# Retention attention and a Fourier-mixing block: a second fold of the channel axis, with step two of the channel transform in four half-contraction products

## The chip, the cores and the metric

The kernel runs on one core of a Trainium2 chip. The core has five engines, each with its own in-order queue of instructions: TensorE (PE in the profile, with its weight loads shown apart as PEld), VectorE (DVE), ScalarE (ACT), GpSimd (POOL) and SyncE (SP, which here only issues DMAs). The metric is the time on the device of one execution in microseconds (us). SBUF is the memory [...]; PSUM is where PE puts its products, and DVE and ACT fetch them from there.

## The reference

For each of 4 batches and 8 heads, with a sequence S of 768 and a head size D of 64:

```python
gamma = 1.0 - 2.0 ** (-5.0 - np.arange(H))
for t in range(S):                               # attention with a decaying state
    state = gamma * state + k[t] v[t]^T          # D x D for each head
    y[t] = scale * q[t] state
x = y.transpose(0, 2, 1, 3).reshape(B, S, H * D) # (4, 768, 512)
mixed = real(fft(fft(x, axis=1), axis=2))        # over the sequence and the channels
u = x + mixed
un = (u - mean(u)) / sqrt(var(u) + 1e-6)         # over the 512 channels
out = u + relu(un @ w_ch1) @ w_ch2               # 512 -> 2048 -> 512
```

(The attention is abbreviated: the head and batch indices are left out.)

## The kernel before

The work is done batch by batch, and everything of PE runs in fp16 with fp32 sums. Per batch there are four head pairs of attention and then the mixing block.

**Attention.** For each head pair, `cast_unit` (L233) turns q, k and v into fp16 on POOL (k also scaled, L253), `t_unit` transposes q and k (L278), `a0_unit` and `a_unit` (L299, L317) form masked products of q and k, `kv_unit` (L335, L345) updates the state, `y_unit` (L366, L370) forms the output in PSUM, and ACT scales it into the fp16 tile `x` (L378).

**The transform.** The sequence is folded first: `fold_s` (L395, DVE) adds and subtracts rows s and s + 384 into the tile `ab`. Then `fold_d` (L405, DVE) folds the channels, d with 512 - d, into `eo`: even sums (e = 0) for the cosine part and odd differences (e = 1) for the sine part, 256 channels in two halves `cb` of 128. `g0_unit` (L443 to L462) treats the channel that has no partner. Step one, `s1_unit` (L425), transforms the sequence: per half and part six matmuls of 193 columns against the tables `csp` or `ssp`, into the PSUM tile `ps1`; ACT (L437) or DVE (L439) copies it as fp16 into `g`, and a DVE copy reversed along the row makes `gr` (L440), which serves the mirrored upper three row blocks. Step two, `s2_unit` (L467), transforms the channels: for each of six row blocks `kb` of 128 rows, two matmuls of 257 columns against the cosine table `cd16` are summed in the first 257 columns of a PSUM tile `pq` (called `psP`), and two of 255 columns against the sine table `sd16` in the other 255 (`psQ`). ACT copies `psQ` to SBUF (`qn`, L488), and DVE writes the sum and the reversed difference of both as the row block of `u` (L491, L493). Then x is added to both halves: the lower one at L497 (DVE in batch 0, POOL later), the upper one at L500 (POOL, but DVE in batch 0 from block 3 on).

**Normalisation and the two dense layers.** DVE takes the mean and variance of u (L510, L511), ACT subtracts the mean into `un` (L506 for the first three blocks of batch 0, with a mean from elsewhere, L512 otherwise), PE transposes it and ACT or DVE copies that as `unT` (`unT_unit`, L533). `h_unit` (L556) makes the hidden layer in 16 groups of four matmuls of 384 columns, `ht` being written alternately by ACT (L560) and DVE (L562); for the lower half of batch 0 `h0_unit` (L573) does so for each row block with matmuls of 128 columns. `ch_unit` (L593) makes the output layer, 192 matmuls of 512 columns a batch in groups of four, and DVE (L597) adds u; then the block is stored.

**What sets the order.** Functions ending in `_unit` return small pieces of work. For each batch the kernel makes streams: the dense layers (`majors`), step two and normalisation of the upper three row blocks (`mix_units`), and, for the next batch, loads, attention (`attn_steps`, L621) and step two of its first three blocks. A stream has a start and an end time in units of a batch, `emit` spaces its pieces evenly between these, sorts all by due time and calls them in that order. The framework's scheduler then orders each engine's queue from that, so an added piece can move others. `attn_steps` has six steps, and the loop runs pair i through them: `y_unit(b, i)` in step i + 2. The first fold, g0 and the two step-one units of half 0 stand at i = 2, that is behind the third head pair; those of half 1 in step 5, behind the fourth.

**Loads and constants.** Loads of q, k, v are issued by SP in turn (`load_unit`, L96). Those of batch 1 wait until the last of eight weight chunks has landed (the argument `after` = 7); the weight chunks are issued from POOL's queue behind the last casts of batch 0 (L607, L615). In `late_consts` (L153) ACT scales a mask eight times, behind the `un` of row block 2 of batch 0. The tables csp, ssp, cd16 and sd16 are computed at the start by DVE and ACT.

**Buffers.** Of PSUM, five buffers (`ps_g`) serve steps one and two and the attention, three (`ps_pm`) the dense layers. `ab` and `eo` have one buffer each.

Of the kernel before, what the change touches and what calls it, by code (L numbers as in the profile page):

```python
# [12 lines left out]
ALU = mybir.AluOpType  # L13
# [21 lines left out]
def kernel(  # L35
# [45 lines left out]
    gk128 = const.tile([P, NHP], f32, tag="gk128")  # L81
    pmask = const.tile([P, 4], f32, tag="pmask")
    sgn = const.tile([P, 1], f32, tag="sgn")

    in_of = {}
    w_dma = []
# [63 lines left out]
    def late_consts():  # L150
        with tc.issue_after(lb[0]["una"].ins):
            for h in range(H):
                nc.scalar.activation(maskp[:, h // 2, h % 2], maskf, AF.Copy, bias=0.0,  # L153
                                     scale=float(gam[h] ** (-P)))
        for j in range(2):
            nc.vector.memset(qzs[j][:, :, 0, D:P], 0.0)
            nc.vector.memset(qzs[j][:, :, 1, 0:D], 0.0)

    m2 = const.tile([P, 1], f32, tag="m2c")
    odd = const.tile([P, 1], f32, tag="oddc")  # L160
# [239 lines left out]
    def fold_d(b, cb):  # L400
# [6 lines left out]
                                        in1=ab[:, :, :, 1, i0:i0 + 128], op=op)  # L407
        return run

    def xmean_unit(kb):  # L410
        def run():
            if kb == 0:
                fd[0]["xm"] = stt.tile([P, 4], f32, tag="xm", name="xm")
            junk = up.tile([P, 2, 257], f16, tag="un16", name="junk")
            nc.scalar.activation(junk, xts[0][:, kb, :, 1:258], AF.Copy, bias=0.0, scale=1.0,
                                 accum_out=fd[0]["xm"][:, kb:kb + 1])
        return run
# [7 lines left out]
    def s1_unit(b, e, cb):  # L425
        def run():
            eo, g, gr = fd[b]["eo"], fd[b]["g"], fd[b]["gr"]
            tab = csp if e == 0 else ssp
            ps = ps_g.tile([P, 2, NK], f32, tag="g", name="ps1", padded_shape=[P, 2, 256])
            for par in range(2):  # L430
                for sb in range(3):
                    nc.tensor.matmul(ps[:, par, :], eo[:, e, par, sb, 128 * cb:128 * cb + 128],  # L432
                                     tab[:, par, sb, :], start=(sb == 0), stop=(sb == 2))
            gi = 2 * e + cb
            dst = g[:, gi].rearrange("p (i t) -> p t i", t=2)
            if e == 0 or b == 0:
                nc.scalar.copy(dst, ps)  # L437
            else:
                nc.vector.tensor_copy(dst, ps)  # L439
            nc.vector.tensor_copy(gr[:, gi], g[:, gi, 384:0:-1])  # L440
        return run

    def g0_unit(b):  # L443
        def run():
            ab = fd[b]["ab"]
            xg = stt.tile([P, 3, 4], f16, tag="xg", name="xg")
            src = ab[:, :, :, 0, 1].rearrange("p a c -> p c a")
            nc.vector.tensor_copy(xg[:, :, 0:2], src)
            nc.vector.tensor_scalar(out=xg[:, :, 2:4], in0=src, scalar1=sgn, scalar2=None,
                                    op0=ALU.mult)  # L450
            ps = ps_g.tile([P, 3, 4], f32, tag="g", name="ps0", padded_shape=[P, 3, 160])
            for kb in range(3):
                for sb in range(3):
                    nc.tensor.matmul(ps[:, kb, :], csn[:, sb, P * kb:P * kb + P], xg[:, sb, :],
                                     start=(sb == 0), stop=(sb == 2))
            gm = stt.tile([P, 3, 4], f32, tag="gm", name="gm")
            nc.vector.tensor_tensor(out=gm, in0=ps,
                                    in1=pmask.unsqueeze(1).to_broadcast([P, 3, 4]), op=ALU.mult)
            g0 = stt.tile([P, 2, 3], f32, tag="g0", name="g0")
            nc.vector.tensor_tensor(out=g0.rearrange("p a k -> p k a"), in0=gm[:, :, 0:4:2],  # L460
                                    in1=gm[:, :, 1:4:2], op=ALU.add)
            fd[b]["g0"] = g0.rearrange("p a k -> p (a k)")  # L462
        return run
# [3 lines left out]
    def s2_unit(b, kb):  # L467
        def run():
# [9 lines left out]
            g0 = f["g0"][:, kb:kb + 1]  # L478
            pq = ps_g.tile([P, DM], f32, tag="g", name="pq")
            psP, psQ = pq[:, 0:257], pq[:, 257:512]  # L480
            for cb in range(2):
                nc.tensor.matmul(psP, gt[:, cb, j0:j0 + P], cd16[:, cb, :],
                                 start=(cb == 0), stop=(cb == 1))
            for cb in range(2):
                nc.tensor.matmul(psQ, gt[:, 2 + cb, j0:j0 + P], sd16[:, cb, 1:256],
                                 start=(cb == 0), stop=(cb == 1))
            qn = qns[kb % 2]
            nc.scalar.copy(qn[:, 1:256], psQ)  # L488
            op_lo = ALU.subtract if mirror else ALU.add
# [131 lines left out]
    def attn_steps(b):  # L621
        steps = []
        for step in range(6):
            un = []
            i = step - 2
            if 0 <= i < 4:
                un.append(y_unit(b, i))
                if i == 2:
                    un += [fold_s(b, 0, 130, 0, 2), fold_d(b, 0), g0_unit(b), s1_unit(b, 0, 0),
                           s1_unit(b, 1, 0)]  # L630
            if step < 4:
                un += [cast_unit(b, step), t_unit(b, step)]
            i = step - 1
# [3 lines left out]
                else:  # L637
                    un += [a_unit(b, i, 0), kv_unit(b, i), a_unit(b, i, 1), a_unit(b, i, 2)]
            if step == 5:
                un += [fold_s(b, 130, 258, 0, 2), fold_d(b, 1), s1_unit(b, 0, 1),  # L640
                       s1_unit(b, 1, 1)]
            steps.append(un)
        return steps
# [44 lines left out]
    for b in range(B):  # L688
# [15 lines left out]
        if b + 1 < B:  # L704
            steps = attn_steps(b + 1)
            if b == 0:
                streams.append(([load_unit(1, i, 7) for i in range(4)], -0.1, 0.0))
                ts = (0.12, 0.22, 0.24, 0.33, 0.42, 0.52, 0.59, 0.67)
            else:
                streams.append(([load_unit(b + 1, i) for i in range(4)], b - 0.3, b + 0.15))  # L710
# [37 lines left out]
```

## Time and profile before

| | us |
|---|---|
| three runs | 275.24, 274.93, 273.69 (median 274.93) |
| the profiled execution | 274.87 |
| its span, from its first instruction to its last | 273.1 |
| PE busy | 243.8 (89%) |
| DVE busy | 179.8 (66%) |
| ACT busy | 116.6 (43%) |
| POOL busy | 71.9 (26%) |

Every duration below is from one profiled execution, whose own time of 274.87 us is 1.77 us longer than its span; the mean granted clock of PE was 0.994 of full. Busy time of PE is the sum of modelled lengths of overlapping matmuls, so 89% doesn't mean that 11% are the whole that could be gained. A line of a timeline gives the start in us, the length in us, engine, line of the code, operation, what is written from what with sizes, and how many instructions are run together in it; in square brackets stand the idle time before it and what ended that. In a group's line, the busy time of all and the mean length of one in ns stand after the first bar, the engine's idle time just before them after the second.

The largest groups by engine are the output layer (L593, 90.4 us on PE), the hidden layer (84.0), DVE's `ht` (30.6) and ACT's (27.3). Of the rest, these are used below:

| group | count | mean of one, ns |
|---|---|---|
| ACT L378, x from PSUM | 32 | 585 |
| POOL L497, add of x | 18 | 637 |
| POOL L500, add of x | 21 | 650 |
| POOL L253, cast and scaling of k | 32 | 623 |
| POOL L258, cast of v | 16 | 834 |
| DVE L491, u from PSUM | 24 | 479 |
| DVE L510, statistics | 21 | 694 |

### The profile page before, as it was taken

To read this page: it belongs to the slowest core of one execution; us is meant where nothing else is said; L and a number is where in the kernel's file an instruction comes from. 1 tells how busy PE (TensorE), PEld (TensorE's weight loads), DVE (VectorE), ACT (ScalarE), POOL (GpSimd) and SP (SyncE) were. 2 spreads that over 40 slices of the span, in tenths; PEclk is the share of its full clock that TensorE was granted. 3 is DMA by queue.
4 is the path that set the end of the run, shared out by engine and by line. 5 is a ranking of instruction groups with operands and counts; after the bars stand their busy time and mean duration, and the time that the engine had idled before them with its cause. 6 is when DMAs were issued, how large, how long until landed. Compare 5 with 4: busy or idle time off the path is not lost.

```text
span 273.1 us, 5125 instructions
## 1 busy us (share of the span) xinstructions
PE 243.8 (89%) x1972; PEld 147.7 (54%) x1972; DVE 179.8 (66%) x458; ACT 116.6 (43%) x238; POOL 71.9 (26%) x122
## 2 busy tenths in 40 slices
PE   1498569998999998889999899989999999999994
PEld 0375458964456453556556544665566445545541
DVE  8964954986677676789778662699687736623411
ACT  3887456665554333546424540452234405402300
POOL 5769002565211214134402220510001303100000
PEclk9999997999999999999999999999999999999999
DMA  8999996999999597958996022144310131112012
GB/s 184 263 245 152 204 204 143 250 245 231 195 202 178 127 211 170 226 111 164 219 212 138 2 49 97 48 106 70 114 41 0 38 97 41 38 58 79 0 38 77
DMA packets 97432, 35.97 MB, mean 132 GB/s; under 512 B 88193, under 2 KB 94337, under 8 KB 97409
## 3 DMA queue, kind: packets, MB, share of 16 engines
q1 hardware_dynamic: 93184, 31.47, 54.2%
q0 software_dynamic: 4224, 4.19, 9.5%
q8 instruction: 15, 0.25, 0.4%
q14 instruction: 9, 0.07, 0.1%
HBM read 27.26 MB, written 6.29 MB: 123 GB/s over the span
## 4 chain that ended last, share of the span: by engine, by line
PE 56%; DVE 23%; ACT 7%; POOL 5%; issue 5%; DMA 1%; POOLq 0%; ACTq 0%; DVEq 0%
PE psc L593 25%; PE psh L556 14%; DVE bst L510 4%; PE ps L432 3%; POOL u L500 3%; PE wkY L366 2%; DVE u L491 2%; POOL u L497 2%; DVE xab L395 2%; PE tq L278 2%; PE psh L573 2%; PE wkY L370 2%; PE wkA L299 2%; DVE ht L562 2%; DVE ob L597 1%
## 5 line engine op out<-in xcount | busy, mean ns | idle before, releaser
L593 PE MATMUL psc<-w,ht 128*128 128x512 f16 x384 | 90.4, 379 | 0.7 <-DVE ht L562 0.7
L556 PE MATMUL psh<-unT,w 128*128 128x384 f16 x448 | 84.0, 326 | 0.9 <-ACT ht L560 0.5
L593 PEld LDWEIGHTS <-ht 128*128 128x128 f16 x384 | 36.0, 98 | 38.4 <-issue 2.0
L556 PEld LDWEIGHTS <-w 128*128 128x128 f16 x448 | 41.6, 98 | 27.4 <-issue 4.6
L560 ACT ACTIVATE ht<-psh 128x384 f16<-128x384 f32 x56 | 27.3, 489 | 61.6 <-PE psh L556 61.6
L562 DVE TENSOR_SCALAR ht<-psh 128x384 f16<-128x384 f32 x56 | 30.6, 547 | 11.8 <-PE psh L556 11.7
L597 DVE SCALAR_TENSOR_TENSOR ob<-psc,stats,u 128x512 f32<-128x512 f32 x24 | 17.9, 746 | 29.0 <-PE psc L593 29.0
L497 POOL TENSOR_TENSOR u<-u,x 128x256 f32<-128x256 f32 x18 | 11.5, 637 | 91.9 <-DVE u L491 89.5
L253 POOL TENSOR_SCALAR kd<-k,gexp 128x384 f16<-128x384 f32 x32 | 19.6, 623 | 30.6 <-DMA k<-in_k_dram 14.3
L512 ACT ACTIVATE un<-u,stats 128x512 f16<-128x512 f32 x21 | 15.1, 721 | 22.9 <-DVE stats L511 22.2
L378 ACT ACTIVATE x<-wkY,gexp 128x384 f16<-128x384 f32 x32 | 17.0, 585 | 16.8 <-PE wkY L370 16.7
L302 DVE SCALAR_TENSOR_TENSOR atm<-wkA,maskf 128x384 f16<-128x384 f32 x32 | 16.9, 547 | 8.7 <-PE wkA L299 8.6
L345 DVE SCALAR_TENSOR_TENSOR s<-s,gk,wkK 128x128 f16<-128x128 f16 x64 | 21.6, 338 | 0.5
L510 DVE BATCH_NORM_STATS2 bst<-u 128x6 f32<-128x512 f32 x21 | 14.6, 694 | 10.1 <-POOL u L500 9.9
L366 PE MATMUL wkY<-s,qTz 64*128 64x64 f16 (+1 forms) x160 | 16.6, 204 | 4.2 <-DVE s L345 2.9
L366 PEld LDWEIGHTS <-qTz 64*128 64x128 f16 (+1 forms) x160 | 10.7, 100 | 14.5 <-issue 9.8
L500 POOL TENSOR_TENSOR u<-u,x 128x256 f32<-128x256 f32 x21 | 13.6, 650 | 16.9 <-DVE u L493 15.7
L258 POOL TENSOR_SCALAR v<-v 128x768 f16<-128x768 f32 x16 | 13.3, 834 | 17.1 <-DMA v<-in_v_dram 7.0
L491 DVE SCALAR_TENSOR_TENSOR u<-pq,g,qn 128x257 f32<-128x257 f32 x24 | 11.5, 479 | 7.4 <-ACT qn L488 7.4
L319 DVE TENSOR_TENSOR atm<-wkA,maskp 128x512 f16<-128x512 f32 x24 | 16.3, 681 | 0.1
L573 PE MATMUL psh<-unT,w 128*128 128x128 f16 x192 | 12.7, 228 | 0.0
L573 PEld LDWEIGHTS <-w 128*128 128x128 f16 x192 | 12.2, 104 | 0.4 <-issue 0.2
(110 smaller groups left out, 294.3 us busy)
## 6 DMA issues: line engine op xcount, KB each, us to landing
q<-in_q_dram SPq DMA_DIRECT2D x16, 384.0 KB, 5.2
k<-in_k_dram SPq DMA_DIRECT2D x16, 384.0 KB, 4.9
v<-in_v_dram SPq DMA_DIRECT2D x16, 384.0 KB, 5.9
out_dram<-ob SPq DMA_DIRECT2D x24, 256.0 KB, 2.2
w<-in_moe_w_ch_dram POOLq DMA_DIRECT2D x8, 512.0 KB, 10.8
unT<-un SPq DMA_TRANSPOSE x12, 2.4
qTz<-q16z SPq DMA_TRANSPOSE x8, 3.8
kT<-kd SPq DMA_TRANSPOSE x8, 2.8
```

What stands on the lines that cost most here:

```text
L253: kc = nc.gpsimd.tensor_scalar(out=kd[:, :, h2, :], in0=k32[:, h2], scalar1=gkd[:, h0 + h2:h0 + h2 + 1], scalar2=1.0, op0=ALU.mult, op1=AL ...
L345: nc.vector.scalar_tensor_tensor(out=s16[:, c], in0=s16[:, c - 1], scalar=gk128[:, hp:hp + 1], in1=wk[:, c - c0], op0=ALU.mult, op1=ALU.add)
L366: nc.tensor.matmul(yk[h2][:, c, :], lhsT, rhs, start=(c == 1), stop=False, skip_group_check=True)
L378: nc.scalar.activation(dst, yk[h2], AF.Copy, bias=0.0, scale=gq8[:, h:h + 1])
L500: eng.tensor_tensor(out=u[:, kb, 256:512], in0=u[:, kb, 256:512], in1=x[:, kb, 1, 257:1:-1], op=ALU.add)
L510: nc.vector.bn_stats(bst, u[:, kb, :])
L556: nc.tensor.matmul(psh, w116[:, cb, fb * P:(fb + 1) * P], unT[:, cb, rt * 384:(rt + 1) * 384], start=(cb == 0), stop=(cb == 3))
L560: nc.scalar.activation(ht16[:, fb, :], psh, AF.Relu, bias=0.0, scale=-1.0)
L562: nc.vector.tensor_scalar(out=ht16[:, fb, :], in0=psh, scalar1=-1.0, scalar2=0.0, op0=ALU.mult, op1=ALU.max)
L573: nc.tensor.matmul(psh[:, f], w116[:, cb, fb * P:(fb + 1) * P], unT[:, cb, kb * P:(kb + 1) * P], start=(cb == 0), stop=(cb == 3))
L593: nc.tensor.matmul(psc, ht16[:, fb, rb3 * P:(rb3 + 1) * P], w216[:, fb, :], start=(fb == 0), stop=(fb == NFB - 1))
L597: nc.vector.scalar_tensor_tensor(out=ob, in0=psc, scalar=lb[b]["st"][:, rb, 3:4], in1=lb[b]["u"][:, rb, :], op0=ALU.mult, op1=ALU.add)
```

## The change

In batches 1 to 3 the 256 folded channels are folded again, d with 256 - d. `fold_e` makes four sets of 128 from `eo`: for the cosine part the sums and the differences (DVE, e = 0), for the sine part the differences and the sums (POOL, e = 1). They stand in the tile `ee`, which takes the buffer of `ab` (same tag). The even and the odd output channels then need only one set each, so a row block of step two is four products with one contraction of 128 each (129 cosine columns of even and 128 of odd number, 127 and 128 sine columns), each started and stopped by itself. Their results are written into `pq` at a stride of two, even and odd interleaved, so that what reads `psP` and `psQ` is unchanged. The tables for that, `t2`, are made once from every second column of cd16 and sd16, with the last row halved or replaced (`half_tables`, POOL). Step one keeps its number and shape of matmuls and reads `ee` instead of `eo`. The channel without a partner in the second fold goes into `g0_unit`, where the copy into `xg` becomes an addition.

Since both halves of `eo` are needed for the second fold, g0 and all four step-one units are moved into step 5, behind both `fold_e`. The stream of `half_tables` has the due time 0.42 of batch 0. Batch 0 itself keeps the old form. In the numbering of the changed kernel, lines after L83 lie later: L254 becomes L272, L405 becomes L423, L500 becomes L547.

```diff
@@ -81,6 +81,8 @@
     gk128 = const.tile([P, NHP], f32, tag="gk128")
     pmask = const.tile([P, 4], f32, tag="pmask")
     sgn = const.tile([P, 1], f32, tag="sgn")
+    last = const.tile([P, 4], f32, tag="last")
+    t2 = const.tile([P, 4, 130], f16, tag="t2")
 
     in_of = {}
     w_dma = []
@@ -155,6 +157,22 @@
         for j in range(2):
             nc.vector.memset(qzs[j][:, :, 0, D:P], 0.0)
             nc.vector.memset(qzs[j][:, :, 1, 0:D], 0.0)
+
+    def half_tables():
+        nc.gpsimd.tensor_scalar(out=last[:, 0:1], in0=icol[:, 0:1], scalar1=float(P - 1),
+                                scalar2=1.0, op0=ALU.is_equal, op1=ALU.mult)
+        for n, (m, a) in enumerate(((-0.5, 1.0), (-1.0, 1.0), (-2.0, 0.0))):
+            nc.gpsimd.tensor_scalar(out=last[:, n + 1:n + 2], in0=last[:, 0:1], scalar1=m,
+                                    scalar2=a, op0=ALU.mult, op1=ALU.add)
+        halve, keep, tail = (last[:, n:n + 1] for n in (1, 2, 3))
+        nc.gpsimd.tensor_scalar(out=t2[:, 0, 0:129], in0=cd16[:, 0, 0:257:2], scalar1=halve,
+                                scalar2=1.0, op0=ALU.mult, op1=ALU.mult)
+        nc.gpsimd.tensor_scalar(out=t2[:, 1, 0:128], in0=cd16[:, 0, 1:257:2], scalar1=keep,
+                                scalar2=tail, op0=ALU.mult, op1=ALU.add)
+        nc.gpsimd.tensor_scalar(out=t2[:, 2, 0:127], in0=sd16[:, 0, 2:256:2], scalar1=keep,
+                                scalar2=1.0, op0=ALU.mult, op1=ALU.mult)
+        nc.gpsimd.tensor_scalar(out=t2[:, 3, 0:128], in0=sd16[:, 0, 1:257:2], scalar1=halve,
+                                scalar2=1.0, op0=ALU.mult, op1=ALU.mult)
 
     m2 = const.tile([P, 1], f32, tag="m2c")
     odd = const.tile([P, 1], f32, tag="oddc")
@@ -407,6 +425,23 @@
                                         in1=ab[:, :, :, 1, i0:i0 + 128], op=op)
         return run
 
+    def fold_e(b, e):
+        def run():
+            eo = fd[b]["eo"]
+            if e == 0:
+                fd[b]["ee"] = fp.tile([P, 4, 2, 3, 128], f16, tag="xab", name="ee",
+                                      padded_shape=[P, 4, 2, 3, 130])
+            ee = fd[b]["ee"]
+            lo, hi = eo[:, e, :, :, 0:128], eo[:, e, :, :, 254:126:-1]
+            eng = nc.vector if e == 0 else nc.gpsimd
+            eng.tensor_tensor(out=ee[:, 2 * e], in0=lo, in1=hi,
+                              op=ALU.add if e == 0 else ALU.subtract)
+            eng.tensor_tensor(out=ee[:, 2 * e + 1], in0=lo, in1=hi,
+                              op=ALU.subtract if e == 0 else ALU.add)
+            if e == 0:
+                eng.tensor_copy(ee[:, 1, :, :, 127:128], eo[:, 0, :, :, 255:256])
+        return run
+
     def xmean_unit(kb):
         def run():
             if kb == 0:
@@ -429,8 +464,9 @@
             ps = ps_g.tile([P, 2, NK], f32, tag="g", name="ps1", padded_shape=[P, 2, 256])
             for par in range(2):
                 for sb in range(3):
-                    nc.tensor.matmul(ps[:, par, :], eo[:, e, par, sb, 128 * cb:128 * cb + 128],
-                                     tab[:, par, sb, :], start=(sb == 0), stop=(sb == 2))
+                    lhsT = fd[b]["ee"][:, 2 * e + cb, par, sb, :] if b else \
+                        eo[:, e, par, sb, 128 * cb:128 * cb + 128]
+                    nc.tensor.matmul(ps[:, par, :], lhsT, tab[:, par, sb, :], start=(sb == 0), stop=(sb == 2))
             gi = 2 * e + cb
             dst = g[:, gi].rearrange("p (i t) -> p t i", t=2)
             if e == 0 or b == 0:
@@ -445,8 +481,13 @@
             ab = fd[b]["ab"]
             xg = stt.tile([P, 3, 4], f16, tag="xg", name="xg")
             src = ab[:, :, :, 0, 1].rearrange("p a c -> p c a")
-            nc.vector.tensor_copy(xg[:, :, 0:2], src)
-            nc.vector.tensor_scalar(out=xg[:, :, 2:4], in0=src, scalar1=sgn, scalar2=None,
+            if b == 0:
+                nc.vector.tensor_copy(xg[:, :, 0:2], src)
+            else:
+                nc.vector.tensor_tensor(out=xg[:, :, 0:2], in0=src,
+                                        in1=ab[:, :, :, 1, 257].rearrange("p a c -> p c a"),
+                                        op=ALU.add)
+            nc.vector.tensor_scalar(out=xg[:, :, 2:4], in0=xg[:, :, 0:2], scalar1=sgn, scalar2=None,
                                     op0=ALU.mult)
             ps = ps_g.tile([P, 3, 4], f32, tag="g", name="ps0", padded_shape=[P, 3, 160])
             for kb in range(3):
@@ -478,12 +519,18 @@
             g0 = f["g0"][:, kb:kb + 1]
             pq = ps_g.tile([P, DM], f32, tag="g", name="pq")
             psP, psQ = pq[:, 0:257], pq[:, 257:512]
-            for cb in range(2):
-                nc.tensor.matmul(psP, gt[:, cb, j0:j0 + P], cd16[:, cb, :],
-                                 start=(cb == 0), stop=(cb == 1))
-            for cb in range(2):
-                nc.tensor.matmul(psQ, gt[:, 2 + cb, j0:j0 + P], sd16[:, cb, 1:256],
-                                 start=(cb == 0), stop=(cb == 1))
+            if b == 0:
+                for cb in range(2):
+                    nc.tensor.matmul(psP, gt[:, cb, j0:j0 + P], cd16[:, cb, :],
+                                     start=(cb == 0), stop=(cb == 1))
+                for cb in range(2):
+                    nc.tensor.matmul(psQ, gt[:, 2 + cb, j0:j0 + P], sd16[:, cb, 1:256],
+                                     start=(cb == 0), stop=(cb == 1))
+            else:
+                for n, (dst, w) in enumerate(((psP[:, 0:257:2], 129), (psP[:, 1:257:2], 128),
+                                              (psQ[:, 1:255:2], 127), (psQ[:, 0:255:2], 128))):
+                    nc.tensor.matmul(dst, gt[:, n, j0:j0 + P], t2[:, n, 0:w],
+                                     start=True, stop=True)
             qn = qns[kb % 2]
             nc.scalar.copy(qn[:, 1:256], psQ)
             op_lo = ALU.subtract if mirror else ALU.add
@@ -626,8 +673,7 @@
             if 0 <= i < 4:
                 un.append(y_unit(b, i))
                 if i == 2:
-                    un += [fold_s(b, 0, 130, 0, 2), fold_d(b, 0), g0_unit(b), s1_unit(b, 0, 0),
-                           s1_unit(b, 1, 0)]
+                    un += [fold_s(b, 0, 130, 0, 2), fold_d(b, 0)]
             if step < 4:
                 un += [cast_unit(b, step), t_unit(b, step)]
             i = step - 1
@@ -637,7 +683,8 @@
                 else:
                     un += [a_unit(b, i, 0), kv_unit(b, i), a_unit(b, i, 1), a_unit(b, i, 2)]
             if step == 5:
-                un += [fold_s(b, 130, 258, 0, 2), fold_d(b, 1), s1_unit(b, 0, 1),
+                un += [fold_s(b, 130, 258, 0, 2), fold_d(b, 1), g0_unit(b), fold_e(b, 0),
+                       fold_e(b, 1), s1_unit(b, 0, 0), s1_unit(b, 0, 1), s1_unit(b, 1, 0),
                        s1_unit(b, 1, 1)]
             steps.append(un)
         return steps
@@ -705,6 +752,7 @@
             steps = attn_steps(b + 1)
             if b == 0:
                 streams.append(([load_unit(1, i, 7) for i in range(4)], -0.1, 0.0))
+                streams.append(([half_tables], 0.4, 0.42))
                 ts = (0.12, 0.22, 0.24, 0.33, 0.42, 0.52, 0.59, 0.67)
             else:
                 streams.append(([load_unit(b + 1, i) for i in range(4)], b - 0.3, b + 0.15))
```

## The prediction

> **What bounds the kernel now.** I read the page first (busy shares, slices, chain of waits, groups), then the timeline around every place where the diff moves an instruction, then the start-to-start spacing of the matmuls on TensorE (PE).
>
> ```profile
> PE   1498569998999998889999899989999999999994
> PEclk9999997999999999999999999999999999999999
> PE 56%; DVE 23%; ACT 7%; POOL 5%; issue 5%; DMA 1%; POOLq 0%; ACTq 0%; DVEq 0%
> L593 PE MATMUL psc<-w,ht 128*128 128x512 f16 x384 | 90.4, 379 | 0.7 <-DVE ht L562 0.7
> ```
>
> The second line is the granted clock. From slice 7 on (41 us) PE is near full: what PE saves there shortens the span, and where PE newly waits it grows. The mean of 379 ns is the length of overlapping instructions; from start to start a 512-column matmul takes 216 ns, a 384-column one 162, a 257-column one of step two 110, a 128-column one with a fresh weight 56 (64 of them in 3.57 us). Those spacings are my prices. PE is already idle beyond them by about 19.6 us between 43 and 269 us, so a new wait may partly replace an old one.
>
> In batch 0 stands the place that matters most:
>
> ```profile
> 44.35 0.75 POOL L500 TENSOR_TENSOR u<-u,x 128x256 f32<-128x256 f32 x1 [2.61 <-DVE u L493]
> 44.68 0.37 SPq L96 DMA_DIRECT2D q<-in_q_dram  x1
> 45.14 0.72 ACT L506 ACTIVATE un<-u,mu 128x512 f16<-128x512 f32 x1
> 45.76 1.69 ACT L153 ACTIVATE maskp<-maskf 128x128 f32<-128x128 f32 x8
> 47.36 0.57 ACT L578 ACTIVATE ht<-psh 128x512 f16<-128x512 f32 x1
> 47.84 0.56 ACT L545 COPY unT<-pst 128x512 f16<-128x512 f16 x1
> 48.19 0.83 POOL L244 TENSOR_SCALAR q<-q 128x768 f16<-128x768 f32 x1 [3.08 <-PE pq L485]
> ```
>
> The add of L500 is for row block 2, the last of three; ACT's `un` waits for it, and behind `un` on ACT's queue stand the eight mask scalings, an `ht` and the `unT` that PE needs next. The cast of batch 1's first q stands behind the add and starts 3.5 us after its load was issued at 44.68, when the last weight chunk had landed.
>
> The hand-over from batch 2 to 3 stands for three such places:
>
> ```profile
> 203.38 0.51 PE L370 MATMUL wkY<-v,atm 128*128 128x64 f16 x12
> 203.73 3.42 PE L556 MATMUL psh<-unT,w 128*128 128x384 f16 x20
> 203.91 1.05 ACT L378 ACTIVATE x<-wkY,gexp 128x384 f16<-128x384 f32 x2
> 205.06 1.02 DVE L395 TENSOR_TENSOR xab<-x 128x768 f16<-128x768 f16 x2
> 206.46 1.02 DVE L405 TENSOR_TENSOR eo<-xab 128x768 f16<-128x768 f16 x2
> 207.07 0.69 PE L432 MATMUL ps<-csp,eo 128*128 128x193 f16 x6
> 210.61 0.39 PE L482 MATMUL pq<-cd,g 128*128 128x257 f16 x2
> 210.83 0.38 PE L485 MATMUL pq<-sd,g 128*128 128x255 f16 x2
> 211.05 2.20 PE L556 MATMUL psh<-unT,w 128*128 128x384 f16 x12
> ```
>
> ACT scales x, DVE folds twice, and 20 hidden-layer matmuls (3.24 us at 162) cover that: PE hardly waits. One unit of step two takes 211.05 - 210.61 = 0.44 us.
>
> **The skill.** "PSUM — Partial Sum Buffer", Specifications, gives 8-byte cachelines and says that any non-contiguous access pattern slows matmuls significantly. No matmul of the trace writes PSUM at a stride, so nothing here confirms it. "SBUF — State Buffer", Who interferes with whom, has VectorE and GpSimd share a port; the trace agrees: a 128x256 add on DVE that takes 0.42 us took 1.04 at 54.14 beside a POOL cast. "GPSIMD Engine Reference", §3.1, prices two-input operations on POOL at about 2.6 cycles an element; the L500 row (650 ns for 256) agrees if most of it is slope. "TensorE: Matmul & The Clock Gate", Part 1, describes a free-running 3.4 us window after which an idle PE is granted half speed; the trace agrees:
>
> ```profile
> 37.92:41.33 3.41, 0.71 (x6) 0.30 (x4) 2.58 (x7) 1.47 (x4) 1.01 (x2) 1.00 1.24 203
> 41.33:44.74 3.41, 3.31 (x28) 3.06 (x29) 1.63 (x4) 1.24 (x4) 0.80 (x2) 0.50 0.59 99
> ```
>
> (from, to, length, busy PE, PEld, DVE, ACT, POOL, clock, DMA share, GB/s): nearly idle in one window, clock 0.50 in the next.
>
> **Step two itself.** Removed per unit: two 257- and two 255-column matmuls, 0.44 us. Added: four of 129, 128, 127 and 128 columns, 0.22 us at 56 each, if writing every second fp32 is free; 18 units (six row blocks, batches 1 to 3) then save 4.0 us. But stride 2 in fp32 is 8 bytes, one line per element where a packed write puts two in a line. I take half rate, 107 ns each, 0.43 us a unit: gain 0.3 us in all. Bounds: 4.0 gained if free; 7.3 lost at quarter rate (0.85 a unit). ACT and DVE read the same packed tile as before.
>
> **Batch 0, order on POOL.** The built order of the changed kernel has on POOL: add of block 0, add of block 1, q cast of batch 1, add of block 2. Before, all three adds stood ahead of the cast. So the add of block 2 now waits for the q load. That load waits for the last weight chunk, and the chunks are issued by POOL behind the casts of batch 0, which the four column operations of `half_tables` hold up: they run from about 20.1, where the cosine table is ready, and move the first kd cast from 20.43 to about 21.35 (each 0.3 to 0.35 by the slopes of POOL's casts). The kd itself is covered (PE takes it at 23.99), and the four single-column operations lie in POOL's wait for k. So: q load at about 45.5, q cast 49.0 to 49.8, add of block 2 to about 50.5, `un` to 51.3, masks (1.69) to 52.9, `ht` 53.4, `unT` of block 1 54.0. PE has the 64 products of block 1 from 48.67 (48.45 and one unit of step two moved ahead) and waits: 5.4 us. Such a gap also empties a clock window; half clock then costs between 0.5 and 2.2, I take 1.0. About 0.5 comes back, since the DVE and ACT work for block 2 catches up. Sum +5.9; bounds 0 and 8.
>
> **The three hand-overs.** g0 and all four step-one units now stand behind the second fold of d and both folds `ee`. From the end of PE's last `wkY`: x and fold_s to 2.2, an `ht`, fold_d done at 3.6, the xg add at 3.75. Then POOL's two folds (768 elements, two inputs): 1.3 to 1.9 each by POOL's rows, 1.66 by the page; I take 1.6. DVE's two folds, 0.55 alone, have two SBUF inputs as well; if POOL holds the port they end at 5.65 and 7.5, the copy of one column at 8.2; without blocking 6.3. PE has 24 + 2 + 4 hidden matmuls, g0 and step one ahead of and between these and would be done with step one at 7.2; with blocking at about 9.8: a wait of 2.6 (0.85 without), 2.85 in batch 1. Against that, old waits in these places go: about 0.3 + 1.2 into batch 1 (waits at 86 and 104 to 109), 1.4 into batch 2 (151), 0.3 into batch 3; what is late next is `un` of the new batch, with eight more output matmuls than now as cover in batch 1. Net: 2.85 + 2 x 2.6 - 3.2 = +4.9; part of the old waits' cause follows as well as part of the new wait overlaps `ht` traffic, so I take +3.5, bounds -0.5 and 5.
>
> **Rest.** POOL is 26% busy and DVE 66%; away from the hand-overs their additions lie beside PE. At the tail one unit of step two is earlier: -0.5 (waits of 0.66 and 0.83 at 231 and 236).
>
> Sum against the profiled execution: 274.87 + 5.9 + 3.5 - 0.3 - 0.5 = 283.5. The median shown is 274.93, the same base.
>
> **Rivals.**
> A, the sum above: 283.5. Own range 281 to 286.
> B, strided writes cost nothing (no row here speaks against it; the page does): 4.0 instead of 0.3, 279.8.
> C, quarter rate: 7.3 lost instead of 0.3 gained, about 291.
> E, DVE's folds are not blocked (that the casts blocked an fp32 add shows blocking, but not for fp16): the hand-overs net about 0: 280.
> F, the batch 0 wait is much smaller, because the load lands sooner than the queue order says, the rest as in A: 277.6.
> D, faster: the saving of PE time in the 18 units of step two, 4.0 us at full rate, is the mechanism; it decides as soon as the new waits add up to less than 4.5. By my sums (5.9, 3.5) the first would have to vanish and the second fall to 1: 274.87 - 4.0 - 0.5 + 1.0 = 271.4. For it: PE is the bound and its work does shrink. Against it: the order on POOL's queue is fixed.
>
> **Numbers.** Chances: A 0.50, B 0.15, E 0.11, C 0.09, F 0.05, D 0.07, near no change 0.03 (full rate and half of the waits). 0.5%, 1.4 us, is about what can be told from no change here. Faster 0.07, same 0.03, slower 0.90. The range 276.5 to 289.5 takes in A, B, E, F; C and D stay out.
>
> **What would show it.** The POOL add of block 2 near 49.8 rather than 44.35, `un` behind it near 50.5, a PE gap from 48.7 to 54, and a second low-clock stretch after it. The spacing of the 128-column `pq` matmuls: 56 (B), 107 (A) or 213 ns (C). At each hand-over POOL's `ee` folds near 1.6 us, DVE's stretched to about twice 0.55, and PE waiting ahead of `ps`. I am wrong if the q cast runs before 45, if the units of step two take half of 0.44 us, or if PE shows no gap before step one.

## The result, and the profile after

The changed kernel took 283.88 us (median of 4 runs, 283.35 to 284.56) against 274.94 us before (4 runs): a ratio of 1.0335, with a 95% interval of 1.0295 to 1.0376. It is slower by 8.9 us. The span of its profiled execution is 281.6 us, 8.5 more than before.

From its page, two of the lines shown before and the engines' shares of the chain of waits:

```profile
PE   1598559498999969998999799999988999899994
PEclk9999986899999999999999999999999999999999
PE 52%; DVE 13%; DMA 12%; POOL 8%; ACT 7%; issue 3%; SPq 3%; POOLq 0%; ACTq 0%
```

Counted from 1, in slices of 7.04 us, PE has a dip to 4 in slice 8 and to 6 in slice 15; the clock is low in slices 6 to 8 (8, 6 and 8 tenths), where before only slice 7 was low (7 tenths). The DMA share of the chain went from 1% to 12%: it now runs through the weight load (6% of the span) and batch 1's first load behind it.

The same matmul of the dense layers was then compared between the two traces, to see where the delay comes in. The first output matmul of batch 0 is at 58.36 before and 6.5 us later after; the first of batch 1 (127.43 before; the output layer has 96 matmuls a batch, not the 192 given above) 6.9; one in the first half's hidden layer of batch 3 (226.94 before) 9.1; the last of all 8.5. So some three quarters of the loss arises in batch 0, ahead of 58 us, in a part of the kernel whose own arithmetic the change doesn't touch.

The timeline of the changed kernel there (start, length, engine, line; idle time before it in brackets):

```profile
45.68 0.37 SPq L98 DMA_DIRECT2D q<-in_q_dram  x1
...
48.91 0.38 PE L527 MATMUL pq<-sd,g16r 128*128 128x255 f16 x2
49.06 0.83 POOL L262 TENSOR_SCALAR q<-q 128x768 f16<-128x768 f32 x1 [7.38 <-DMA q<-in_q_dram]
...
49.86 0.63 POOL L547 TENSOR_TENSOR u<-u,x 128x256 f32<-128x256 f32 x1
...
50.53 0.72 ACT L553 ACTIVATE un<-u,mu 128x512 f16<-128x512 f32 x1 [5.35 <-POOL u L547]
...
51.15 1.69 ACT L155 ACTIVATE maskp<-maskf 128x128 f32<-128x128 f32 x8
51.30 0.40 PE L588 MATMUL pst<-ident,un 128*128 128x128 f16 x4 [2.01 <-ACT un L553]
...
52.75 0.58 ACT L625 ACTIVATE ht<-psh 128x512 f16<-128x512 f32 x1
53.23 0.57 ACT L592 COPY unT<-pst 128x512 f16<-128x512 f16 x1
...
53.84 3.40 PE L620 MATMUL psh<-unT,w 128*128 128x128 f16 x33 [1.71 <-ACT unT L592]
```

The add of row block 2 (L547, L500 before) began at 44.35 before and begins at 49.86 now. Its operands had long been there: POOL stood 7.38 us waiting for the q load, whose cast is ahead of it in the queue. The rest follows down ACT's queue to PE's hidden layer.

The hand-over from batch 2 to 3 in the same timeline:

```profile
209.49 0.55 DVE L609 TENSOR_SCALAR ht<-psh 128x384 f16<-128x384 f32 x1
209.52 0.49 ACT L607 ACTIVATE ht<-psh 128x384 f16<-128x384 f32 x1 [0.87 <-PE psh L603]
209.72 1.51 POOL L437 TENSOR_TENSOR ee<-eo 128x768 f16<-128x768 f16 x1 [19.67 <-DVE xg L487]
209.96 1.29 DVE L490 TENSOR_SCALAR xg<-xg,sgn 128x6 f16<-128x6 f16 x1
211.16 0.55 DVE L437 TENSOR_TENSOR ee<-eo 128x768 f16<-128x768 f16 x1
211.18 1.90 POOL L439 TENSOR_TENSOR ee<-eo 128x768 f16<-128x768 f16 x1
211.31 0.38 PE L495 MATMUL ps<-xg,csn 128*128 128x4 f16 x9 [1.23 <-DVE xg L490]
...
211.81 1.69 DVE L439 TENSOR_TENSOR ee<-eo 128x768 f16<-128x768 f16 x1
...
213.97 0.17 DVE L442 COPY ee<-eo 128x6 f16<-128x6 f16 x1
...
214.19 0.69 PE L469 MATMUL ps<-csp,ee 128*128 128x193 f16 x6 [0.99 <-DVE ee L442]
```

Two operations of DVE are stretched, each begun while one of POOL's folds was running: the sign of six elements takes 1.29 us (0.22 in batch 2) and the second fold 1.69 (the first, 0.55). POOL's second fold, begun just after DVE's first, is stretched too (1.90 against 1.51). PE waits 1.23 us for the sign and 0.99 for what stands behind DVE's second fold.

### The profile page after: what moved, and what is told of

The parts are those of the page before. It is cut to its first block, busy times and chain, and to the rows that moved or that the text cites. A ratio compares the mean times of both kernels' runs of the same rounds, so it can differ in the third digit from the quotient of the medians.

```text
span 281.6 us, 5150 instructions
## 1 busy us (share of the span) xinstructions
PE 245.3 (87%) x1972; PEld 150.6 (53%) x1972; DVE 186.2 (66%) x467; ACT 116.3 (41%) x238; POOL 86.0 (31%) x136
## 4 chain that ended last, share of the span: by engine, by line
PE 52%; DVE 13%; DMA 12%; POOL 8%; ACT 7%; issue 3%; SPq 3%; POOLq 0%; ACTq 0%
PE psc L640 26%; PE psh L603 14%; DMA w<-in_moe_w_ch_dram 6%; SPq L98 3%; DVE bst L557 3%; DMA v<-in_v_dram 3%; PE psh L620 3%; POOL u L547 2%; DMA qTz<-q16z 2%; PE wkY L384 2%; DVE ht L609 2%; ACT un L559 2%; PE wkY L388 2%; POOL u L544 1%; PE wkA L335 1%
## 5 line engine op out<-in xcount | busy, mean ns | idle before, releaser
L640 PE MATMUL psc<-w,ht 128*128 128x512 f16 x384 | 92.1, 379 | 1.2 <-DVE ht L609 0.8
L603 PEld LDWEIGHTS <-w 128*128 128x128 f16 x448 | 42.7, 100 | 24.3 <-issue 0.9
L271 POOL TENSOR_SCALAR kd<-k,gexp 128x384 f16<-128x384 f32 x32 | 20.7, 657 | 33.4 <-PE wkK L353 26.2
L384 PE MATMUL wkY<-s,qTz 64*128 64x64 f16 (+1 forms) x160 | 15.9, 203 | 3.0 <-DVE s L363 1.9
L547 POOL TENSOR_TENSOR u<-u,x 128x256 f32<-128x256 f32 x21 | 13.5, 643 | 13.9 <-DVE u L540 13.9
L620 PE MATMUL psh<-unT,w 128*128 128x128 f16 x192 | 15.4, 256 | 1.7 <-ACT unT L592 1.7
L620 PEld LDWEIGHTS <-w 128*128 128x128 f16 x192 | 15.0, 119 | 2.0 <-issue 1.9
```

Source lines behind the costliest of these rows:

```text
L271: kc = nc.gpsimd.tensor_scalar(out=kd[:, :, h2, :], in0=k32[:, h2], scalar1=gkd[:, h0 + h2:h0 + h2 + 1], scalar2=1.0, op0=ALU.mult, op1=AL ...
L384: nc.tensor.matmul(yk[h2][:, c, :], lhsT, rhs, start=(c == 1), stop=False, skip_group_check=True)
L547: eng.tensor_tensor(out=u[:, kb, 256:512], in0=u[:, kb, 256:512], in1=x[:, kb, 1, 257:1:-1], op=ALU.add)
L603: nc.tensor.matmul(psh, w116[:, cb, fb * P:(fb + 1) * P], unT[:, cb, rt * 384:(rt + 1) * 384], start=(cb == 0), stop=(cb == 3))
L620: nc.tensor.matmul(psh[:, f], w116[:, cb, fb * P:(fb + 1) * P], unT[:, cb, kb * P:(kb + 1) * P], start=(cb == 0), stop=(cb == 3))
L640: nc.tensor.matmul(psc, ht16[:, fb, rb3 * P:(rb3 + 1) * P], w216[:, fb, :], start=(fb == 0), stop=(fb == NFB - 1))
```

## The experiments

Two theories of the loss stood against others. First: that POOL's order in batch 0 costs about 6 us, against the delay of the loads by the new tables. Second: that POOL's folds cost the rest at the hand-overs, against the later place of step one, and against step two having become dearer. All times are medians; every ratio is to the kernel before, run on the same chip beside it. The differences given in us are of the medians; worked out from the ratios, each comes out within 0.5 us of that.

**Order on POOL.** The edit:

```diff
-            eng.tensor_tensor(out=u[:, kb, 256:512], ...
+            lb[b]["hi", kb] = eng.tensor_tensor(out=u[:, kb, 256:512], ...
...
+                    if (b, i) == (1, 0):
+                        es.enter_context(tc.issue_after(lb[0]["hi", 2].ins))
```

> The changed kernel with one edge more: POOL's first q cast of batch 1 stands behind the add of row block 2 of batch 0. Theory (the order on POOL's queue costs the batch 0 part): the add ends near 45 instead of 50.5, PE has no gap between 48 and 54 and no second half-clock stretch after it, and the time is 277.3 to 278.5 (283.9 less 5.4 to 6.6). Rival (the order is harmless, the late weight chunks hold batch 1's load and its attention anyway, so that the wait only moves on): 281 or more.

Measured: 278.10 us, ratio 1.0114 (1.0082 to 1.0145). Its timeline:

```profile
44.38 0.75 POOL L549 TENSOR_TENSOR u<-u,x 128x256 f32<-128x256 f32 x1 [2.29 <-DVE u L542]
...
45.34 0.37 SPq L98 DMA_DIRECT2D q<-in_q_dram  x1
...
48.72 1.50 PE L622 MATMUL psh<-unT,w 128*128 128x128 f16 x24
...
48.78 0.83 POOL L264 TENSOR_SCALAR q<-q 128x768 f16<-128x768 f32 x1 [3.65 <-PE pst L590]
```

The load of batch 1 is still late (issued at 45.34, before at 44.68) and its cast at 48.78, but PE starts the next hidden matmuls at 48.72 without the wait. The clock is low in one stretch only (42.14 to 45.56), and the second one of the changed kernel is gone. The order was 5.8 us of the 8.9.

**Tables behind the add,** the cast left ahead of it: `half_tables` is put inside the same kind of edge, `with tc.issue_after(lb[0]["hi", 2].ins):`.

> The changed kernel with the operations of half_tables behind the add of row block 2 on POOL; the q cast still stands ahead of that add. Theory (the order is the cost, the tables only shift the load): the q load is issued about 0.9 us sooner, the add follows it, and the time falls by 0.5 to 1.2, to 282.7 to 283.4. Rival (the tables in POOL's queue are the cost themselves): 277 to 278.5.

Measured: 282.85 us, ratio 1.0279 (1.0243 to 1.0314): 1.0 us less, with intervals that overlap. Its trace shows the same 1.0 us: with the cast still ahead of it, the add begins at 48.86 instead of 49.86, and PE's two waits behind it are 1.17 and 1.70 us instead of 2.01 and 1.71. The tables are not the wait; they lengthen it.

**Packed writes in step two.**

```diff
-                for n, (dst, w) in enumerate(((psP[:, 0:257:2], 129), (psP[:, 1:257:2], 128),
-                                              (psQ[:, 1:255:2], 127), (psQ[:, 0:255:2], 128))):
+                for n, (dst, w) in enumerate(((psP[:, 0:129], 129), (psP[:, 129:257], 128),
+                                              (psQ[:, 0:127], 127), (psQ[:, 127:255], 128))):
```

> The changed kernel with the four products of step two written packed, even columns after each other and odd ones after each other, instead of at a stride of two; it leaves out the interleaving, so the channels of u stand in another order. Theory (a strided write runs at half rate): the 128-column matmuls of step two go from 108 to 56 ns from start to start, a unit from about 0.40 to 0.22 us, and 18 units save up to 3.2 us: 280.7 to 282.5, less where PE waits for something else. Rival (108 ns is the price of a fresh weight or of separate starts, not of the stride): spacing stays at 108 and the time at 283.9.

Measured: 282.47 us (281.33 to 283.60), ratio 1.0274 (1.0230 to 1.0317). One unit of step two and what follows it on PE, first in the changed kernel, then packed, both from the timeline of PE alone:

```profile
219.66 0.60 PE L532 MATMUL pq<-t,g 128*128 128x129 f16 x4
220.06 0.85 PE L603 MATMUL psh<-unT,w 128*128 128x384 f16 x4
...
223.70 0.59 PE L640 MATMUL psc<-w,ht 128*128 128x512 f16 x2 [0.21 <-ACT ht L607]
```

```profile
219.18 0.40 PE L532 MATMUL pq<-t,g 128*128 128x129 f16 x4
219.41 0.81 PE L603 MATMUL psh<-unT,w 128*128 128x384 f16 x4
...
220.76 0.81 PE L603 MATMUL psh<-unT,w 128*128 128x384 f16 x4 [0.48 <-DVE ht L609]
...
223.40 0.81 PE L640 MATMUL psc<-w,ht 128*128 128x512 f16 x3 [0.33 <-ACT ht L607]
```

The unit takes 220.06 - 219.66 = 0.40 us at a stride and 219.41 - 219.18 = 0.23 packed. From start to start, the strided matmuls take 109 ns, except mostly the first of a unit (129 columns), 69; packed, 56 to 60. A fresh weight is in both, so it is the stride. But 18 x 0.17 = 3.1 us of PE time became 1.4 us in the medians, with overlapping runs, and 0.5 in the two spans: in the second fence PE catches up with DVE and ACT (0.48, 0.33), which write `ht`. That this is where the rest of the saving goes is shown at this one place and not summed over the 18.

**All second folds on DVE.**

```diff
-            eng = nc.vector if e == 0 else nc.gpsimd
+            eng = nc.vector
```

> The changed kernel with all four second folds on DVE, none on POOL. Theory (POOL's two folds of 1.5 to 1.9 us each are what step one waits for, and they hold DVE's small xg operation and folds back): DVE needs 4 x 0.55 in a row, no operation is stretched, PE waits about 1 us less to 2 us less at each hand-over, and the time is 279 to 281.5. Rival (DVE is the scarce engine there, and POOL relieved it): 284 to 285.

Measured: 279.08 us, ratio 1.0155 (1.0116 to 1.0193), 4.8 us less. The timeline at the same hand-over:

```profile
208.21 0.22 DVE L490 TENSOR_SCALAR xg<-xg,sgn 128x6 f16<-128x6 f16 x1
208.34 0.56 DVE L437 TENSOR_TENSOR ee<-eo 128x768 f16<-128x768 f16 x1
208.48 0.36 PE L495 MATMUL ps<-xg,csn 128*128 128x4 f16 x9
...
208.97 0.56 DVE L439 TENSOR_TENSOR ee<-eo 128x768 f16<-128x768 f16 x1
...
210.07 0.56 DVE L439 TENSOR_TENSOR ee<-eo 128x768 f16<-128x768 f16 x1
...
210.23 0.69 PE L469 MATMUL ps<-csp,ee 128*128 128x193 f16 x6
210.75 1.19 PE L469 MATMUL ps<-ssp,ee 128*128 128x193 f16 x12
```

Nothing is stretched, and four folds on one engine end before two on each did: 210.63 - 208.21 = 2.4 us from the sign, against 214.14 - 209.96 = 4.2 to the one-column copy in the changed kernel. The run takes away two things at once, the stretching and POOL's own length (two folds take 3.0 us on POOL even undisturbed, as in batch 2; four on DVE take 2.2); how the 4.8 us divide between them is not shown.

**The move alone,** on the kernel before:

```diff
-                    un += [fold_s(b, 0, 130, 0, 2), fold_d(b, 0), g0_unit(b), s1_unit(b, 0, 0),
-                           s1_unit(b, 1, 0)]
+                    un += [fold_s(b, 0, 130, 0, 2), fold_d(b, 0)]
...
-                un += [fold_s(b, 130, 258, 0, 2), fold_d(b, 1), s1_unit(b, 0, 1),
-                       s1_unit(b, 1, 1)]
+                un += [fold_s(b, 130, 258, 0, 2), fold_d(b, 1), g0_unit(b), s1_unit(b, 0, 0),
+                       s1_unit(b, 0, 1), s1_unit(b, 1, 0), s1_unit(b, 1, 1)]
```

> The kernel before with g0 and the four step-one units moved into step 5 behind the second fold of d, as in the change, and nothing else of it. Theory (at the hand-overs the second folds are the cost and the move alone only trades waits): 274 to 276. Rival (having step one late is itself the cost of the hand-overs): 277 to 279.

Measured: 274.29 us, ratio 0.9965 (0.9948 to 0.9983). A later step one doesn't cost, it gains 1.0 us. Its three adds of batch 0 stand ahead of the cast (the last at 43.08, the cast at 48.33).

**The tables alone,** on the kernel before: `half_tables`, its two tiles and its stream added, used by nothing.

> The kernel before with half_tables added in its place and used by nothing; the adds of batch 0 keep their order on POOL. Theory (the tables alone only delay the weight chunks and batch 1's loads by about 0.9 us, and these have slack when the add does not wait for them): 274.5 to 275.8. Rival (the delay goes through to the end): 275.8 to 277.

Measured: 274.98 us, ratio 0.9991 (0.9969 to 1.0013). The delay of the loads has slack as long as no add waits for them. Here too the order of POOL in batch 0 is unchanged (the last add at 42.76, the cast at 49.20), so neither the move nor the tables alone brings the exchange about. Which parts of the change do it together, no run shows.

**Both repairs together,** the edits of the first and the fourth experiment:

> The changed kernel with both edits together: the q cast behind the add of row block 2, and all second folds on DVE. Theory (two separate places, so the gains of 5.8 and 4.8 add up): 273 to 274.3. Rival (what one edit frees the other uses up, or the tail takes it): 275.5 to 278.

Measured: 272.00 us, ratio 0.9894 (0.9869 to 0.9918). The two gains add up: by ratio 1.0335 - 0.0221 - 0.0180 = 0.9934 was to come. The measured one is lower still, and the time is below the range expected, but the intervals of the three ratios in that sum are wide enough for it. It is faster than the kernel before, by 1.1%.

**Without the second folds,** with the order edge:

```diff
-                un += [fold_s(b, 130, 258, 0, 2), fold_d(b, 1), g0_unit(b), fold_e(b, 0),
-                       fold_e(b, 1), s1_unit(b, 0, 0), s1_unit(b, 0, 1), s1_unit(b, 1, 0),
+                un += [fold_s(b, 130, 258, 0, 2), fold_d(b, 1), g0_unit(b), s1_unit(b, 0, 0), s1_unit(b, 0, 1), s1_unit(b, 1, 0),
...
-                    lhsT = fd[b]["ee"][:, 2 * e + cb, par, sb, :] if b else \
+                    lhsT = fd[b]["ee"][:, 2 * e + cb, par, sb, :] if False else \
```

> The changed kernel with the q cast behind the add of row block 2, and without the second folds: step one reads eo as before the change, the four products of step two stay, so the transform of batches 1 to 3 is left incomplete. Theory (the folds are what is late at the hand-overs): against 278.1 with the folds it gains 3.5 to 5.5, 272.6 to 274.6. Rival (what step one waits for is the move, or step two has become dearer): 276.5 or more.

Measured: 271.16 us, ratio 0.9869 (0.9818 to 0.9920). Against 278.10 with the folds split over two engines, the folds cost 6.9 us; against 272.00 with all on DVE only 0.8, within the intervals. Its four runs lie far apart (269.68 to 273.64), so the 6.9 is known to some 2 us; it is more than the 3.5 to 5.5 expected. The late step one and the strided step two are still in this kernel, and it is 3.6 us faster than the kernel before: neither is the cost.

**Three more.** To both repairs the late tables were added, then the packed cosine part, which DVE reads back as pairs:

```diff
-(psP[:, 0:257:2], 129), (psP[:, 1:257:2], 128)
+(psP[:, 0:129], 129), (psP[:, 129:257], 128)
...
+                nc.vector.scalar_tensor_tensor(
+                    out=u[:, kb, 0:256].rearrange("p (i t) -> p i t", t=2),
+                    in0=pq[:, 0:258].rearrange("p (t i) -> p i t", t=2)[:, 0:128], scalar=g0,
+                    in1=qn[:, 0:256].rearrange("p (i t) -> p i t", t=2), op0=ALU.add, op1=op_lo)
```

(the upper half likewise, with i running down.)

> Order edge, all second folds on DVE, and half_tables behind the add of row block 2 on POOL. Theory (with the order edge in place the tables' delay of batch 1's load has slack, as the tables alone cost nothing): the ratio to the kernel before within 0.3% of the 0.989 without this edit. Rival (the 0.9 us of load time come through): 0.986 or less.

Measured: 272.30 us, ratio 0.9893 (0.9865 to 0.9921): no difference, as from the tables alone.

> The kernel of e9 with the cosine part of step two written packed (129 even columns, then 128 odd), and DVE reading it back interleaved by pairs; the sine part stays at a stride of two. Two 128-column matmuls a unit go from 69 and 109 to about 57 each: 18 x 0.06 = 1.1 us of PE time. Theory (in e3 the PE time saved went mostly into waits for the chain from u to un, so little of it reaches the end): 0 to 0.5 us faster than e9. Rival (with the long waits gone PE is the bound and gets all of it): 1 us or more faster. If DVE's paired reading takes longer than 0.48 us an operation, it can be slower by up to 1.

Measured: 271.59 us, ratio 0.9872 (0.9843 to 0.9900). DVE's paired reading costs nothing (474 ns against 478). The 0.7 us lies between the two expectations and inside the intervals; how much of PE's 1.1 us comes through stays open. It is faster than both kernels, as are the two runs to which it adds.

The third took the small operation from under POOL's folds, on the kernel of the first experiment:

```diff
-            nc.vector.tensor_scalar(out=xg[:, :, 2:4], in0=xg[:, :, 0:2], scalar1=sgn, scalar2=None,
-                                    op0=ALU.mult)
+            if b == 0:
+                nc.vector.tensor_scalar(out=xg[:, :, 2:4], in0=xg[:, :, 0:2], scalar1=sgn,
+                                        scalar2=None, op0=ALU.mult)
+            else:
+                nc.scalar.activation(xg[:, :, 2:4], xg[:, :, 0:2], AF.Copy, bias=0.0, scale=sgn)
```

> The kernel of e1 with the second small xg operation (the sign) of batches 1 to 3 on ACT instead of DVE, where POOL's fold holds it for 1.2 to 1.3 us in batches 1 and 3. Theory (POOL's folds hold DVE's folds just the same, so PE's wait only moves from g0 to the first csp matmul): 277.3 to 278.3 against 278.1. Rival (the held-up small operation is itself the wait): 275.5 to 276.5, 2 x 1.2 less.

Measured: 280.61 us, ratio 1.0197 (1.0164 to 1.0229), 2.5 us slower, which neither expected. The timeline of its hand-over to batch 1:

```profile
92.72 1.51 POOL L439 TENSOR_TENSOR ee<-eo 128x768 f16<-128x768 f16 x1 [3.63 <-DVE xg L489]
93.02 1.62 DVE L439 TENSOR_TENSOR ee<-eo 128x768 f16<-128x768 f16 x1
93.02 0.36 PE L500 MATMUL ps<-xg,csn 128*128 128x4 f16 x9
...
94.18 1.82 POOL L441 TENSOR_TENSOR ee<-eo 128x768 f16<-128x768 f16 x1
...
94.56 1.86 DVE L441 TENSOR_TENSOR ee<-eo 128x768 f16<-128x768 f16 x1
...
94.70 0.69 PE L471 MATMUL ps<-csp,ee 128*128 128x193 f16 x6 [1.08 <-DVE ee L439]
...
96.69 1.07 PE L471 MATMUL ps<-csp,ee 128*128 128x193 f16 x6 [1.09 <-DVE ee L444]
```

With the sign gone, DVE's first fold meets POOL's first one and its second meets the second: both are stretched, where in the kernel of the first experiment only the second was (1.69 in all three batches, the first 0.55). The sign was stretched there in all three batches as well (1.23, 1.23 and 1.29), not in two as I had expected. PE's wait moves from g0 to step one, as the theory had it, and doesn't become longer: in the three hand-overs the two waits are 2.17, 2.56 and 1.94 us, against 2.21, 2.54 and 2.22 in the kernel of the first experiment. So the 2.5 us lie elsewhere. The windows at this hand-over show one part, first in this run, then in the first experiment (clock: third column from the end):

```profile
96.83:100.24 3.41, 3.41 (x22) 3.22 (x21) 1.86 (x7) 0.60 (x1) 0.00 (x0) 0.50 0.65 104
```

```profile
96.83:100.24 3.41, 3.07 (x29) 2.56 (x30) 1.95 (x8) 0.60 (x1) 0.00 (x0) 1.00 0.66 108
```

PE is busy all through this window and is granted half the clock, so up to half of 3.41, 1.7 us, is lost. Up to this hand-over the two runs go side by side (within 0.1 us), and at the first output matmul of batch 1 this one is 1.7 us later. Another 2 us arise between about 174 and 185, where operations stand in another order than in the first experiment; 0.7 comes back at the tail. What causes these stays open, and whether the other executions had the low clock here as well is not on record.

## Why the prediction was right

The forecast was 283.5 us with a range of 276.5 to 289.5; the median is 283.88. The two main steps held: the exchanged add and cast, and the blocked folds at the hand-overs. That the sum came within 0.4 us is partly luck, since errors in their sizes cancel.

- **Batch 0, +5.9.** In place by 58 us there were 6.5 us more; taking the exchange back gave 5.8 us. The cast was put at 49.0 to 49.8 and came at 49.06; the add was to end at about 50.5, and ended at 50.49; `unT` was put at 54.0, PE started at 53.84. PE's wait itself was put too large, at 5.4 us instead of some 4.0 (2.17 and 1.87 from one matmul's start to the next, less its usual spacing; the brackets count from a modelled end), since PE came there later (its last product ahead of the wait began at 49.02) and did the transposes of block 2 and a unit of step two in between. The half clock cost more: the first low stretch lasted to 47.4 instead of 44.8 (1.2 us; the last section shows that this comes and goes between runs and isn't tied to the change), and another, 54.2 to 57.6, followed the gap as foretold (about 1.7 instead of 1.0). The windows of the trace show both stretches; clock is the first of the three last columns:

```profile
44.74:48.15 3.41, 3.41 (x42) 3.41 (x40) 0.69 (x1) 0.44 (x1) 0.00 (x0) 0.62 0.42 125
...
54.98:58.40 3.42, 3.42 (x42) 3.42 (x40) 2.29 (x6) 0.65 (x2) 1.99 (x3) 0.62 1.22 267
```

- **Hand-overs, +3.5 net; with step two's -0.3 and the tail's -0.5, +2.7.** The trace has 8.5 - 6.5 = 2.0; the first experiment, without the exchange, is 3.3 us above the kernel before. By the output matmuls that follow each hand-over (127.43, 184.48 and 214.19 before), the delay goes from 6.5 to 6.9, 6.7 and 9.5, and by 237.83 it is 8.5. So the one into batch 3 costs 2.9 us net, those into batches 1 and 2 next to nothing. The forecast has them at about 1.4, 1.2 and 2.3 before its last allowance, and the 1.0 that comes back behind them is twice the 0.5 put down for the tail. The new waits were well sized where the blocking came about: in batch 3, counted from the end of the last `wkY` at about 206.0, DVE's folds were to end at 5.65 and 7.5 and the copy at 8.2; they ended at 5.7, 7.5 and 8.1. PE's two waits there are 1.39 + 1.16 = 2.55 us against 2.6, again from start to start less the spacing. Unforeseen was that the first stretched operation would be the sign of six elements, and that in batch 2 POOL was late itself, behind a v cast that waited 8.30 us for its load, so that nothing of DVE's folds was stretched and PE waited for POOL's own:

```profile
157.29 0.69 PE L469 MATMUL ps<-ssp,ee 128*128 128x193 f16 x6 [0.74 <-POOL ee L437]
158.75 0.69 PE L469 MATMUL ps<-ssp,ee 128*128 128x193 f16 x6 [0.77 <-POOL ee L439]
```

The stretching agrees with "SBUF — State Buffer", Who interferes with whom, in the Trainium skill, by which VectorE and GpSimd block each other at a port that they share; the runs show who is stretched and when, and not the port. With the folds off POOL the time fell by 4.8 us. The estimate from "GPSIMD Engine Reference", §3.1, gave 1.66 us for a fold on POOL, I took 1.6, the trace has 1.50 for an undisturbed one.

- **Step two, -0.3.** The strided writes are slower, as "PSUM — Partial Sum Buffer", Specifications, in the Trainium skill says without a figure: 109 ns from start to start against 56 to 60 packed, about half the rate, as I had taken it. With the 69 ns of most first matmuls the unit is 0.40 us and PE saves 18 x 0.044 = 0.8 us, of which no share could be told apart in the end time.
- **The rivals.** B's time (279.8) was wrong by its own sum, not only by its premise: with packed writes, where the full rate is there, 3.1 us less of PE brought 1.4. The sum took each microsecond of PE for one of the span. The other rivals fell in the trace: C with the 109 ns, F with the start of the add, E with the stretched folds, and D with both of its conditions.

The forecast's gross sums can be set beside the kernel without second folds. It put the new waits at 2.85 + 2 x 2.6 = 8.05 us and what goes against them at 3.2 + 0.5 + 0.3 = 4.0; the runs have 6.9 for the folds and 3.6 (2.2 to 5.0) for the rest. The last allowance, from 4.9 to 3.5, was a judgement that no run tests. What the 3.6 us consist of is known in part: the move alone gains 1.0, which I had only as a way to lose cover, and the tables gain nothing. What else makes the kernel of the move alone (0.9965) slower than that with four products of step two and no folds (0.9869) was not separated: PE's 0.8 us are not enough for it.

## What to carry to other kernels

Compare the order of each engine's queue, also far from the edit: here most of the loss was one cast that stood ahead of one add in a batch that the change leaves as it was, and one edge took it back. Giving half of a two-input elementwise job to POOL was no split here: four folds on DVE end sooner than two on DVE and two on POOL, which is slower at each and was stretched together with DVE. And PE time saved in short units between long chains is not span time until the engines that feed PE are shown to keep up. Last, when two runs differ by 1 or 2 us, look at the clock of each window before explaining the difference by waits.

## What the runs showed of the hardware that was not expected

- A matmul of 128 columns into PSUM at a stride of two fp32 takes 108 to 110 ns from start to start, 56 to 60 packed. The first strided one behind a packed one takes only 67 to 70 (129 columns in the changed kernel, 127 in the run with the cosine part packed); where a strided unit follows another directly, as twice in the changed kernel, its first takes 110 as well.
- A DVE operation on six fp16 elements a partition took 1.23 and 1.29 us instead of 0.22 while a POOL fold of 768 elements was running; its own size gives no hint of that. An fp16 fold of 768 elements took up to 1.86 us on DVE instead of 0.55, and POOL's own 1.90 instead of 1.50. Of the folds and the sign in the timelines above, the operation that began while the other engine's fold was well under way is the stretched one, on DVE and on POOL alike.
- The half clock behind the same idle gap of PE (3.0 to 3.1 us from start to start, ahead of the first transposes of `un`) lasts 3.41 us in some runs and 6.83 in others: in the former it begins between 41.0 and 42.2 us (the kernel before, the first experiment, packed writes, folds on DVE, no second folds, the sign on ACT), in the latter between 40.2 and 40.5 (the changed kernel, tables behind the add, both repairs and the two runs built on these). With the move alone and with the tables alone no half clock follows the gap; theirs lasts from about 22 to 36. The changed kernel, that with packed writes and that with all folds on DVE have the same queue order there and yet not the same length, so these 1.2 us of PE time belong to no edit.
